# A decode step of windowed attention with a gated MLP: w_q loaded in three transfers instead of one, fewer transfers at the end

## The chip, the core and the metric

One Trainium2 chip, one of its cores, one launch. The metric is device time in microseconds (us) of the whole program. The core has a matrix engine (PE, with its weight loads shown as PEld), three engines for elementwise work (DVE, ACT, POOL), SP, which here only issues transfers, and 16 DMA engines that move data between the chip's memory (HBM) and the 128 partitions of on-chip memory (SBUF).

## What is computed

Two sequences, one new token each, D = 512. Cut to what matters:

```python
xn = layernorm(x)                                  # x: 2 x 1 x 512
q = (xn @ wq).reshape(2, 1, 32, 128)               # wq: 512 x 4096
k, v = the last 4096 rows of k_cache, v_cache      # 2 x 8 heads x 32768 x 128, each head for 4 heads of q
s = softmax(q @ k.T * 128 ** -0.5) @ v @ wo        # wo: 4096 x 512
z = gelu(xn @ w_in); z1, z2 = halves of z          # w_in: 512 x 1792
g = silu((z1 * (w_sp * layernorm(z2) + b_sp)) @ w_out)   # w_out: 896 x 512
out = x + s * g
```

All is float32. The weights and the 4096 rows of 16 heads of K and of V make 89.4 MB, each byte of which is used once.

## The kernel before

All large loads go through one ring in SBUF of four slots of 4 MB (line 80, 32 KB in each partition). `enqueue` (line 85) puts a load in line for the next slot or slots; `advance` (line 92) marks slots as free and issues the loads whose slots are free, in order, from SP's queue. So the loads are issued in a fixed order, each as soon as the work that read its slot before is done: w_q in two slots (line 120), w_in (121) and w_out (122) in one each, then in turn a K and a V load of 4 MB for each of eight units (lines 155 to 159; a unit is two KV heads of one sequence), then w_o in three slots (lines 179 and 180).

A large load puts 128 rows into 128 partitions. `load_rows` (line 112) gives partition p four rows of w_q that lie next to each other in HBM, one run of 64 KB; 16 DMA engines with 8 of the 128 partitions each carry it. `load_blocks` (line 164) does the same for w_o, which is cut in 32 blocks: block j holds row 32p + j of w_o in partition p, 2 KB each, 256 KB in all. The first slot has 16 blocks in one transfer, the second 8, and the third is cut in transfers of 4, 1, 1, 1 and 1 blocks, so that the last matmuls wait for little. Once 16 blocks are in line, x is loaded a second time for the final addition, into rows of `x4` 16 partitions apart, one transfer for each sequence (lines 173 to 175). `by_group` (line 129) is the same layout of all eight rows in HBM as one pattern; the output is stored through it (line 555).

The order of the work on the engines is the program's order, kept by the helper on line 27 (so most records of the trace have its line, 37). ACT loads x (line 109) for the layernorm; lines 219 to 232 make `xnT`. The 32 matmuls of q (lines 263 to 271; the profile counts each as two) read all of w_q with all 128 partitions as the contraction, so they begin when all of w_q has landed; `advance(0, 1)` after them issues the first K loads. Then the gated MLP is done as far as `gate` (lines 293 to 363). The units follow (lines 486 to 515): DVE transposes K into `kt`, PE forms the scores, ACT the exponentials, PE the product with V (`acc`). Lines 516 to 531 finish the last two units into `oT`, the attention's result in columns.

The end is lines 534 to 555. PE multiplies `oT` with blocks 0 to 27 of w_o into `part`; ACT copies it to `parts`; PE adds blocks 28 and 29, then the shares in `parts`, then blocks 30 and 31 into `so`, in this order. DVE multiplies with `gate` and adds `x4`, and SP stores the result.

A transfer signals that it has landed through one of eight semaphores, which all transfers of the program take in turn; one that gets a semaphore again waits until the transfer that had it before has landed.

Of the kernel before, what the change touches and what calls it, by code (L numbers as in the profile page):

```python
# [14 lines left out]
P = 128  # L15
HQ, DH = 32, 128
G = 4
# [25 lines left out]
def kernel(  # L43
# [14 lines left out]
    pe, dve, act, sp = (InOrder(tc, e) for e in (nc.tensor, nc.vector, nc.scalar, nc.sync))  # L58
    B, _, D = x.shape
# [5 lines left out]
    KT = D // P  # L65
# [19 lines left out]
    def enqueue(load, count=1):  # L85

        at = turns[0] % 4
        turns[0] += count
        queue.append((load, range(at, at + count)))
        advance()  # L90

    def advance(*slots):
        for n in slots:
            free[n] = True
        while queue and all(free[n] for n in queue[0][1]):
            load, at = queue.pop(0)
            for n in at:
                free[n] = False
            load(ring[:, at[0] * SLOT : (at[-1] + 1) * SLOT], at[0])

    def const(name, *shape):
        return cst.tile([P, *shape], F32, tag=name, name=name)
# [7 lines left out]
    weight = {}  # L110

    def load_rows(name, w, k):
        def load(t, at):
            n = k * w.shape[1]
            sp.dma_start(t[:, :n], w.rearrange("(p k) f -> p (k f)", p=P))
            weight[name] = t[:, :n].rearrange("p (k f) -> p k f", k=k)

        return load

    enqueue(load_rows("q", wq, KT), 2)  # L120
    enqueue(load_rows("in", w_in, KT))
    enqueue(load_rows("out", w_out, FT))
    win, wout, wqt = (weight[n] for n in ("in", "out", "q"))
# [5 lines left out]
    def by_group(t):  # L129

        return bass.AP(tensor=t.tensor, offset=t.offset, ap=[[DC, G], [D, B], [1, DC]])
# [32 lines left out]
    def load_blocks(piece):  # L164
        def load(t, at):
            t = t.rearrange("p (j d) -> p j d", d=D)
            a = 0
            for n in piece:
                j = len(blocks)
                sp.dma_start(t[:, a : a + n, :], wo_v[:, j : j + n, :])  # L170
                blocks.extend((t, a + i) for i in range(n))
                a += n
            if len(blocks) == 16:
                for b in range(B):
                    sp.dma_start(x4[16 * b : P : 32, :], x[b].rearrange("o (g c) -> (o g) c", g=G))

        return load

    for piece in ((16,), (8,), (4, 1, 1, 1, 1)):
        enqueue(load_blocks(piece))  # L180


# [8 lines left out]
    x4 = const("x4", DC)  # L191
# [72 lines left out]
    for k in range(KT):  # L264
        for r in range(2):
            for g in range(G):
                c = (r * G + g) * 512
# [82 lines left out]
    for j in range(FT):  # L350
        g = j % G
# [111 lines left out]
    def gather(b):  # L463

        hq = sb.tile([P, 32], F32, tag="hq", name=f"hq{b}")
        by_d = col[0][32 * b : 32 * b + 32, :].rearrange("p (j d) -> p d j", j=NCH)
        for e in range(4):
            dve.reduce_sum(hq[32 * e : 32 * e + 32, :], by_d[:, 32 * e : 32 * e + 32, :], axis=AX.X)
        t = bank(f"oT{b}", "acc")[:, :32]
        pe.matmul(t, perm, hq, start=True, stop=True)  # L470
        return t
# [56 lines left out]
    t = gather(last.b)  # L528
# [7 lines left out]
    for n in range(EARLY):  # L536
        t, a = blocks[n]
        g = n % G
# [4 lines left out]
    for n in range(EARLY, 32):  # L543
        if n == LATE:
            spread_quarters(so, parts, start=False, stop=False)
        t, a = blocks[n]
# [37 lines left out]
```

## Time and profile before

| | us |
|---|---|
| median of 3 runs (217.4 to 217.73) | 217.57 |
| the profiled execution | 218.1 |
| its span, first to last instruction | 216.3 |
| PE busy in it | 149.5 |
| DVE busy | 107.1 |
| ACT busy | 43.5 |

The profile is of one execution, and its span starts at 0. Busy time is that of instructions; a DMA engine's time stands apart, as the share of the 16 engines' span. A chain entry "DMA tile<-tensor" lasts from the issue of a transfer to its landing; "issue" is time in which an engine waited for nothing that the profile shows. The granted clock is the part of its full rate that PE was given. Where bytes per time are shown for very short slots, a packet is counted whole in the slot in which it starts.

### The profile page before, as it was taken

The page shows a single profiled execution, that of the slowest core. Times are in us where ns is not written, and L with a number is a line of the kernel's source. Part 1 is how long each engine was busy: PE and PEld are TensorE (multiplying, and loading weights), DVE is VectorE, ACT ScalarE, POOL GpSimd, SP SyncE. Part 2 cuts the span into 40 slices and gives each one's busy share as a digit, 9 for nine tenths or more (in the row PEclk, how much of TensorE's full clock was granted, in tenths as well). Part 3 has the DMA queues.
Part 4 walks back from the last instruction along what each step waited for, and adds up shares of the span by engine and source line. Part 5 has one row for each costly group of instructions (what it writes and reads, how often), then busy time and mean ns, then how long its engine had stood idle before and what let it go on. Part 6 is the DMA issues. An engine that isn't in the chain of part 4 may idle for free.

```text
span 216.3 us, 2178 instructions
## 1 busy us (share of the span) xinstructions
PE 149.5 (69%) x848; PEld 41.7 (19%) x848; DVE 107.1 (50%) x160; ACT 43.5 (20%) x107; POOL 4.2 (2%) x22
## 2 busy tenths in 40 slices
PE   0100796417199499499599779829968977987793
PEld 0100222111012122122122122202212221222221
DVE  2400016430895890792694449487459089233101
ACT  5000000241022214212411511411241151241001
POOL 6100000000000000000000000000000000000000
PEclk9999996965559979969969969976996997999678
DMA  9988999999999999999999999999999999999980
GB/s 376 400 388 388 424 427 458 445 424 430 442 414 454 394 467 403 448 418 454 418 435 430 418 448 412 439 424 448 412 448 421 436 424 436 430 430 409 417 346 17
DMA packets 3789, 89.54 MB, mean 414 GB/s; under 512 B 434, under 2 KB 450, under 8 KB 964
## 3 DMA queue, kind: packets, MB, share of 16 engines
q1 hardware_dynamic: 3772, 89.40, 96.5%
q8 instruction: 7, 0.11, 0.2%
q14 instruction: 2, 0.02, 0.0%
q10 hardware_dynamic: 8, 0.00, 0.0%
HBM read 89.40 MB, written 0.00 MB: 413 GB/s over the span
## 4 chain that ended last, share of the span: by engine, by line
PE 55%; DMA 25%; DVE 15%; ACT 2%; issue 2%; DVEq 0%; ACTq 0%
PE s L37 15%; DMA ring<-in_A_wo_dram 15%; PE sh L37 12%; PE acc L37 11%; DMA ring<-in_A_wq_dram 10%; DVE kt L37 8%; PE q_ps L37 4%; PE part L37 4%; PE col L37 2%; PE z L37 2%; PE y L37 2%; PE mo L37 1%; DVE gate L37 1%; DVE u L37 1%; DVE qm L37 1%
## 5 line engine op out<-in xcount | busy, mean ns | idle before, releaser
L37 DVE STREAM_TRANSPOSE kt<-ring 128x2048 f32<-128x2048 f32 x32 | 72.1, 2284 | 10.7 <-DMA ring<-in_A_k_cache_dram 10.7
L37 PE MATMUL sh<-kt,qbd 128*32 128x512 f32 x256 | 41.9, 666 | 24.4 <-DVE kt L37 24.4
L37 PE MATMUL s<-shs,add_dq 128*128 128x512 f32 x64 | 41.5, 755 | 0.0
L37 ACT ACTIVATE shs<-sh 128x512 f32<-128x512 f32 x32 | 19.1, 597 | 97.2 <-PE sh L37 97.2
L37 PE MATMUL acc<-ring,pT 128*32 128x512 f32 x256 | 33.1, 646 | 0.0
L37 PE MATMUL q_ps<-ring,xnT 128*32 128x512 f32 x64 | 9.3, 746 | 15.5 <-DMA ring<-in_A_wq_dram 15.5
L37 DVE TENSOR_REDUCE m<-s 128x2 f32<-128x512 f32 x8 | 5.5, 685 | 22.5 <-PE s L37 22.5
L37 PEld LDWEIGHTS s<-shs,add_dq 128*128 128x128 f32 x64 | 11.2, 219 | 27.6 <-issue 23.2
L37 PEld LDWEIGHTS sh<-kt,qbd 128*32 128x32 f32 x256 | 7.2, 112 | 43.8 <-issue 35.3
L37 PEld LDWEIGHTS acc<-ring,pT 128*32 128x32 f32 x256 | 7.8, 119 | 25.5 <-issue 19.4
L37 DVE STREAM_TRANSPOSE qT<-q_ps 128x512 f32<-128x512 f32 x2 | 1.4, 718 | 22.8 <-PE q_ps L37 22.7
L37 PE MATMUL part<-ring,oT 128*32 128x512 f32 x56 | 9.2, 825 | 1.4 <-DMA ring<-in_A_wo_dram 1.4
L37 ACT ACTIVATE o<-acc,diag 128x128 f32<-128x128 f32 x30 | 8.6, 374 | 4.9 <-PE acc L37 4.9
L37 ACT ACTIVATE p<-s,nb 128x256 f32<-128x256 f32 x16 | 7.6, 487 | 6.8 <-DVE nb L37 6.6
L37 ACT ACTIVATE zs<-z 128x448 f32<-128x448 f32 x1 | 0.5, 544 | 34.5 <-PE z L37 34.5
L37 PE MATMUL col<-o,sel 128*32 128x512 f32 x14 | 7.3, 601 | 0.0
L37 PEld LDWEIGHTS q_ps<-ring,xnT 128*32 128x32 f32 x64 | 2.5, 134 | 21.4 <-issue 21.4
L37 PE MATMUL y<-ring,hT 128*32 128x512 f32 x14 | 3.6, 1058 | 3.8 <-DVE hT L37 3.8
L37 DVE TENSOR_TENSOR res<-so,gate 128x128 f32<-128x128 f32 x1 | 0.3, 292 | 11.7 <-PE so L37 11.7
L37 DVE STREAM_TRANSPOSE pT<-p 128x512 f32<-128x512 f32 x8 | 5.4, 674 | 1.2 <-ACT p L37 1.2
L37 ACT ACT_TABLE_LOAD x4 | 5.1, 1283 | 1.9 <-issue 1.9
L37 PE MATMUL xnT_ps<-ident,xn 2*128 2x2 f32 x4 | 0.6, 252 | 6.8 <-DVE xn L37 6.8
(112 smaller groups left out, 64.0 us busy)
## 6 DMA issues: line engine op xcount, KB each, us to landing
ring<-in_A_k_cache_dram SPq DMA_DIRECT2D x8, 4096.0 KB, 19.0
ring<-in_A_v_cache_dram SPq DMA_DIRECT2D x8, 4096.0 KB, 25.0
ring<-in_A_wo_dram SPq DMA_DIRECT2D x1, 4096.0 KB, 31.8
ring<-in_B_w_in_dram SPq DMA_DIRECT2D x1, 3584.0 KB, 30.0
ring<-in_A_wo_dram SPq DMA_DIRECT2D x1, 2048.0 KB, 27.2
ring<-in_B_w_out_dram SPq DMA_DIRECT2D x1, 1792.0 KB, 33.9
ring<-in_A_wo_dram SPq DMA_DIRECT2D x1, 1024.0 KB
ring<-in_A_wo_dram SPq DMA_DIRECT2D x4, 256.0 KB, 17.2
```

What stands on the lines that cost most here:

```text
L37: return self.tc.keep_in_program_order(call(*args, **kwargs))
```

## The change

w_q is loaded in three transfers. The first has partitions 0, 4, 8, ..., the second 2, 6, 10, ..., the third all odd ones: 32, 32 and 64 of the 128 rows of 64 KB, which makes 2, 2 and 4 rows for each of 16 DMA engines. x for the result comes in one transfer of eight rows. In the third slot of w_o, the first two of the four single blocks come in one transfer.

```diff
-    enqueue(load_rows("q", wq, KT), 2)
+    def load_q(t, at):
+
+        rows, n = wq.rearrange("(p k) f -> p (k f)", p=P), KT * wq.shape[1]
+        for first, step in ((0, 4), (2, 4), (1, 2)):
+            sp.dma_start(t[first:P:step, :n], rows[first:P:step])
+        weight["q"] = t[:, :n].rearrange("p (k f) -> p k f", k=KT)
+
+    enqueue(load_q, 2)
...
             if len(blocks) == 16:
-                for b in range(B):
-                    sp.dma_start(x4[16 * b : P : 32, :], x[b].rearrange("o (g c) -> (o g) c", g=G))
+                sp.dma_start(x4[0:P:16, :], by_group(x))
...
-    for piece in ((16,), (8,), (4, 1, 1, 1, 1)):
+    for piece in ((16,), (8,), (4, 2, 1, 1)):
         enqueue(load_blocks(piece))
```

The program has as many transfers as before: two more at its start, one fewer for x and one fewer for w_o.

## The prediction

> **What bounds the kernel now.** I read the page first: the span, the strip of 40 slices and the queues.
>
> ```profile
> span 216.3 us, 2178 instructions
> PEclk9999996965559979969969969976996997999678
> DMA  9988999999999999999999999999999999999980
> q1 hardware_dynamic: 3772, 89.40, 96.5%
> ```
>
> The reader is to see one digit repeated: the 16 DMA engines are busy from the first slice to the last but one, and queue 1, SP's own, has 96.5% of their time. No compute engine comes near. So I ask next whether the DMA engines ever wait. The table by stage answers it (after the times: busy time of PE, PEld, DVE, ACT and POOL, then the granted clock, the DMA share and GB/s; a packet counts whole where it starts, so shares over 1 in a short stretch only mean that many started there).
>
> ```profile
> 1.10:1.70 0.60, 0.00 (x0) 0.00 (x0) 0.26 (x1) 0.00 (x0) 0.59 (x3) 1.00 0.07 7
> 1.70:2.10 0.40, 0.00 (x0) 0.00 (x0) 0.31 (x2) 0.23 (x1) 0.40 (x5) 1.00 3.46 1147
> 2.10:2.50 0.40, 0.00 (x0) 0.00 (x0) 0.00 (x0) 0.40 (x1) 0.40 (x3) 1.00 4.02 1475
> 5.00:22.40 17.40, 0.61 (x4) 0.55 (x4) 2.30 (x13) 0.33 (x2) 0.76 (x4) 1.00 0.99 429
> 31.00:200.00 169.00, 129.37 (x690) 34.54 (x683) 102.11 (x138) 39.96 (x102) 0.00 (x0) 0.85 1.00 431
> 207.00:209.60 2.60, 2.60 (x24) 0.72 (x20) 0.00 (x0) 0.00 (x0) 0.00 (x0) 0.75 1.02 392
> 209.60:211.70 2.10, 2.10 (x36) 0.84 (x28) 0.00 (x0) 0.13 (x1) 0.00 (x0) 1.00 0.44 167
> ```
>
> Before 1.7 us nothing of queue 1 moves; from 5 to 200 us the share is 0.99 to 1.00 at 429 to 431 GB/s; from 209.6 us it falls, because engines finish one by one. **The kernel is a full pipe with a start of about 2 us and an end of about 4.5 us**, and only three things can move its time: when the pipe starts, what it loses on the way, and what comes after the last bytes. The chain in order of time shows the two ends (start, length, what):
>
> ```profile
> 0.74 22.00 DMA ring<-in_A_wq_dram
> 22.73 0.14 issue
> 22.87 9.32 PE q_ps L37 x64
> ...
> 170.30 31.85 DMA ring<-in_A_wo_dram
> 202.15 0.14 issue
> 202.28 9.21 PE part L37 x56
> ...
> 211.57 0.61 ACT parts L37
> ...
> 212.22 0.91 PE so L37 x24
> ...
> 213.15 0.30 DVE res L37
> ...
> 213.48 0.29 DVE res L37
> ```
>
> w_q is first in the pipe, and its landing lets PE begin. The 16-block load of w_o lands at 202.15 us; from there PE, ACT and DVE run to the end. An earlier pipe moves both.
>
> **w_q in three transfers.** The bytes stay the same, and all of w_q is still needed before the first q matmul, since the contraction runs over all partitions. So nothing is gained by an early part. What can be gained is the start. Below, the first packets of the pipe: the stretch 1.7 to 2.5 us in slots of 20 ns (3277 is one 64 KB packet that starts there), and then the second packets, 4.7 to 5.6 us in slots of 22.5 ns.
>
> ```profile
> GB/s 0 3277 3277 3277 0 0 0 0 0 0 3277 0 3277 3277 0 0 0 3277 0 0 0 3277 3277 3277 0 3277 0 0 3277 0 0 0 3277 0 3277 0 3277 3277 0 0
> GB/s 0 0 0 0 0 0 2913 0 2913 0 2913 5825 0 0 2913 2913 5825 2913 2913 0 5825 0 0 0 2913 0 0 0 0 2913 0 0 0 0 2913 0 0 0 0 0
> ```
>
> The 16 engines do not start together: the first at 1.72, the last at 2.44 us, about 48 ns apart. Each then has 8 rows of w_q waiting. 128 rows in 0.72 us are 5.6 ns a row, as if the rows were handed out one engine after another. The only other start on an empty queue is the output's, 8 rows (512 B packets, slots of 57.5 ns from 214 us):
>
> ```profile
> GB/s 0 0 0 0 0 0 0 0 0 0 0 0 0 0 0 0 0 9 53 9 0 0 0 0 0 0 0 0 0 0 0 0 0 0 0 0 0 0 0 0
> ```
>
> Its 12 packets (8 of data, 4 of semaphores) start within three slots, so 8 rows take some 0.1 us, at most 14 ns a row. With 32 rows in the first transfer the handing out should take 32 x 5.6 = 0.18 to 32 x 14 = 0.45 us. The last engine then starts at 1.9 to 2.17 instead of 2.44 us: 0.27 to 0.54 us earlier; the mean engine gains half of that.
>
> Is the head start kept? The second packets start between 4.83 and 5.48 us, 0.65 apart where the first were 0.72 apart. A 64 KB row takes 65536 B / (429/16 GB/s) = 2.44 us, yet from the first starts to the second it is some 3 us: the first bytes come about 0.6 us late, for a reason that no row shows and that an earlier start may not move. So part of the head start can be lost there. Bounds: 0 (all lost) to 0.54 us. Every landing waits for the slowest engine, so its gain counts more than the mean's; I take **0.30 us**, a little under the middle of the last engine's gain.
>
> What else the split issues:
>
> ```profile
> 0.74 0.38 SPq L37 DMA_DIRECT2D ring<-in_A_wq_dram  x1
> 1.18 0.41 SPq L37 DMA_DIRECT2D ring<-in_B_w_in_dram  x1
> 1.63 0.48 SPq L37 DMA_DIRECT2D ring<-in_B_w_out_dram  x1
> 28.77 3.99 SPq L37 DMA_DIRECT2D ring<-in_A_k_cache_dram  x2
> ```
>
> Two more issues on SP, 0.44 us each, put w_in and w_out 0.9 us later in SP's queue, to 2.1 and 2.5 us. Their cover is w_q's data, which keeps the engines busy to 22 us. The second transfer is issued near 1.2 us, and the first keeps each engine for two rows, 4.9 us; so no engine runs dry between them. ACT's load of x shares these first microseconds; its consumers (layernorm, xnT) are done by 8 us and PE waits for w_q until 22.7. The first q matmul has three landings to wait for in place of one; two come long before. Should that add 0.1 us on PE, q ends later and so do the k loads queued behind it at 28.77 us, while the pipe still has w_out to move: nothing.
>
> **w_o: two single blocks in one transfer.** A 2 KB row takes longer than its bytes: at the singles the table has 392 GB/s at a share of 1.02, so 2048 B / (384/16) = 85 ns a row, against 76 ns at 431 GB/s, 9 ns for each packet. Joining two blocks saves 8 packets an engine: **0.07 us** at the last landing. Blocks 28 and 29 now land together, at the time of 29; PE takes them after its 28 blocks of `part`, at 211.26 us in the row below, later than that. The bounds are 0 and 0.07.
>
> **x for the result** is 8 rows of 512 B either way, one issue fewer. It is needed 40 us later by the last addition: nothing.
>
> **A wait goes.** SP's own waits and the last issue of w_o (the last column is issue to landing):
>
> ```profile
> SPq L37 <- DMA ring<-in_A_wo_dram: 7.6, 1, 7.6
> ring<-in_A_wo_dram SPq DMA_DIRECT2D x1, 256.0 KB, 10.0
> 211.26 0.63 PE L37 MATMUL so<-ring,oT 128*32 128x128 f32 x16
> ```
>
> The last block's issue stands 7.6 us until the 16-block load has landed, since the transfers take eight semaphores in turn and it is the eighth after that load. With two transfers fewer at the end it looks back to a V load that has long landed and is issued near 194 us. But at 202.16 us the queue still held up to 15 blocks, 3.9 MB or 9 us, and the block landed 10.0 us after its issue, in the stream's own order. So this too is worth nothing; at most a few hundredths if the tail has a gap that I can't see.
>
> **Sum.** 0.30 + 0.07 = 0.37 us. The profiled execution took 218.1 us (span 216.3, 1.8 around it) and would take 217.7; the median of the runs, 217.57, is 0.5 lower, and from it I get **217.2 us**. No step works on 0.2% (0.44 us, about what a measurement of this kernel can tell from no change) with certainty: the likeliest gain is just under it.
>
> **Rivals.**
>
> *The rows of a small transfer meet at one door (slower).* Every large transfer in this trace goes to all 128 partitions, and every engine keeps its pace of 27 GB/s. No row shows a transfer to 32 partitions with a step. If there two engines write through one entrance of SBUF at the same time, each goes at half pace. w_q's 8.39 MB take 19.5 us at 431 GB/s; at half pace the pipe is late by up to 19.5 us, by 4.9 if only the first 32 rows suffer; everything behind shifts, since the pipe has no slack: 222.5 to 237 us. It decides as soon as w_q lands over 0.5 us later than 22.7. [...] Chance 0.17.
>
> *The head start is lost.* The first packets wait longer for their bytes instead of starting earlier, or the start of an engine doesn't depend on the rows. 0.0 to 0.15 us remain: 217.5. For it: the second packets' spread above. Chance 0.18.
>
> *A new wait.* If the three transfers, whose partitions interleave, were held apart (each waiting for the one before to land), each would cost a start of 1.0 us from issue to first packet and up to 0.7 for the last engine: 2.0 to 3.4 us, 219.6 to 221. Against it: the two loads of x interleave in the same way and follow each other without a wait.
>
> ```profile
> 170.69 1.21 SPq L37 DMA_DIRECT2D x<-in_A_x_dram  x2
> ```
>
> Two issues of 0.6 us in 1.21 us leave no room for one. Chance 0.03.
>
> *More than the head start.* PE runs the 28 blocks at a granted clock of half for two steps:
>
> ```profile
> 201.45:204.86 3.41, 2.58 (x15) 0.74 (x19) 0.05 (x1) 0.00 (x0) 0.00 (x0) 0.50 0.97 411
> 204.86:208.28 3.42, 3.42 (x24) 0.93 (x20) 0.00 (x0) 0.00 (x0) 0.00 (x0) 0.50 0.99 405
> ```
>
> The first step is 76% busy (2.58 of 3.41) and the clock stays low; an earlier landing fills it further, and if that lifts the clock at 204.86 us, `part` ends 1.7 us earlier. Then the last block's landing (202.16 + 10.0 = 212.16 us) sets the end: its 8 matmuls are half of the 0.62 us after 212.47, so they start at 212.78 now, 0.6 later than they could. The median lies 0.5 below the profiled execution, so most runs may have this already. I give 216.8 and a chance of 0.07.
>
> **How the numbers follow.** The forecast has 0.55: gains of 0.15 to 0.7 us, 216.9 to 217.4. The range runs from the last rival's 216.7 to 217.9, a little above the lost head start and the spread of the runs; the door and the new wait, 0.20 together, are left out, as their times are far off. Faster by over 0.2%: 0.25 of the 0.55 and the 0.07, 0.32. Within: 0.29 and 0.17, 0.46. Slower: the 0.20, and 0.02 from the edges, 0.22.
>
> **What would show it.** Right: first packets spread over 0.2 to 0.45 us, w_q landed by 22.45, the 16 blocks of w_o near 201.85, the last single block issued near 194 us with no landing waited for. Wrong: w_q landing later than 22.7 with a DMA share near 0.5 before it (the door), gaps in SP's first issues (a new wait), or an earlier first packet with w_q's landing unmoved (head start lost).

## The result: slightly slower, and a start that comes later

| | before | after |
|---|---|---|
| median of 22 runs, us | 217.57 | 217.96 |
| ratio of the times, 95% interval | | 1.002, 1.001 to 1.0029 |
| the profiled execution, us | 218.1 | 217.93 |
| its span, us | 216.3 | 216.0 |

The change costs 0.39 us, 0.1 to 0.3%; the forecast was a gain of 0.37, and the time lies 0.06 us above the range. Two profiles alone would have told the opposite: the profiled execution of before took 0.5 us more than the median. So the times are compared by medians, and the profiles only at places where executions hardly differ, above all the first microseconds. Two executions in a slower state of the chip, one of `covered` below and one of before beside `late_start`, are left out of the medians and ratios. A ratio is estimated by itself and need not be the quotient of the medians beside it.

There the difference is plain. First SP's issues after the change (start, length, times merged), then the stretches around the first packets, as they were read before, then the first packets of 64 KB in slots of 20 ns from 1.7 us.

```profile
0.74 1.89 SPq L37 DMA_DIRECT2D ring<-in_A_wq_dram  x3
2.67 0.59 SPq L37 DMA_DIRECT2D ring<-in_B_w_in_dram  x1
3.30 0.43 SPq L37 DMA_DIRECT2D ring<-in_B_w_out_dram  x1
```

```profile
1.70:2.10 0.40, 0.00 (x0) 0.00 (x0) 0.31 (x2) 0.17 (x1) 0.40 (x5) 1.00 1.01 328
2.10:2.50 0.40, 0.00 (x0) 0.00 (x0) 0.36 (x1) 0.40 (x1) 0.40 (x3) 1.00 5.95 1966
5.00:22.40 17.40, 0.61 (x4) 0.55 (x4) 2.28 (x13) 0.00 (x0) 0.76 (x4) 1.00 1.01 437
31.00:200.00 169.00, 128.59 (x683) 33.25 (x676) 101.20 (x135) 39.64 (x102) 0.00 (x0) 0.86 1.00 431
```

```profile
GB/s 0 0 0 0 0 0 0 0 0 0 0 0 0 0 0 0 0 0 0 6554 3277 9830 0 0 3277 3277 0 0 0 0 0 6554 0 0 3277 3277 0 0 3277 3277
```

The reader is to see that the first packet starts at 2.08 us, where it was 1.72: not earlier but **0.36 us later**. And the last two of the 16 engines start at 2.70 and 2.74 us, after the end of the row, where the last was at 2.44: the starts spread over 0.66 us, where it was 0.72. Three issues in 1.89 us are 0.63 from one to the next, where w_q's one issue took 0.38. From 5 us on the stream is as full and as fast as before. The chain in time order has the two ends:

```profile
0.74 0.57 SPq L37
1.37 0.57 SPq L37
1.98 20.97 DMA ring<-in_A_wq_dram
23.09 8.39 PE q_ps L37 x64
```

```profile
195.37 16.91 DMA ring<-in_A_wo_dram
212.28 0.04 issue
212.33 0.47 PE so L37 x8
```

w_q lands at 1.98 + 20.97 = 22.95 us (before 22.74), 0.21 us later, and the last block at 212.28 (before 212.16). Why w_q's landing moved by less than the first packet no row shows. The last block is now issued at 195.37 us without waiting for the first part of w_o; `tail_only` below shows that this brings nothing the runs can tell, as forecast.

### The profile page after: what moved, and what is told of

Read it like the earlier page. It is cut to its first block, busy times and chain, and to the rows that moved or that the text cites. A ratio compares the mean times of both kernels' runs of the same rounds, so it can differ in the third digit from the quotient of the medians.

```text
span 216.0 us, 2181 instructions
## 1 busy us (share of the span) xinstructions
PE 147.8 (68%) x848; PEld 39.8 (18%) x848; DVE 107.3 (50%) x160; ACT 43.5 (20%) x107; POOL 4.2 (2%) x22
## 4 chain that ended last, share of the span: by engine, by line
DMA 40%; PE 34%; DVE 20%; issue 2%; ACT 2%; SPq 1%; DVEq 0%
DMA ring<-in_A_k_cache_dram 23%; DVE kt L37 13%; DMA ring<-in_A_wq_dram 10%; PE sh L37 9%; PE s L37 9%; DMA ring<-in_A_wo_dram 8%; PE acc L37 6%; PE q_ps L37 4%; PE y L37 2%; PE z L37 1%; SPq L37 1%; PE mo L37 1%; PE col L37 1%; DVE gate L37 1%; DVE u L37 1%
## 5 line engine op out<-in xcount | busy, mean ns | idle before, releaser
L37 DVE STREAM_TRANSPOSE kt<-ring 128x2048 f32<-128x2048 f32 x32 | 72.3, 2287 | 23.6 <-DMA ring<-in_A_k_cache_dram 23.3
L37 PE MATMUL s<-shs,add_dq 128*128 128x512 f32 x64 | 39.4, 723 | 0.0
L37 PE MATMUL acc<-ring,pT 128*32 128x512 f32 x256 | 36.2, 698 | 0.0
L37 PE MATMUL q_ps<-ring,xnT 128*32 128x512 f32 x64 | 8.4, 681 | 16.1 <-DMA ring<-in_A_wq_dram 16.1
L37 PEld LDWEIGHTS s<-shs,add_dq 128*128 128x128 f32 x64 | 10.4, 203 | 28.4 <-issue 24.0
L37 PEld LDWEIGHTS acc<-ring,pT 128*32 128x32 f32 x256 | 8.4, 128 | 27.6 <-issue 24.7
L37 DVE STREAM_TRANSPOSE qT<-q_ps 128x512 f32<-128x512 f32 x2 | 1.4, 718 | 22.5 <-PE q_ps L37 22.4
L37 PE MATMUL part<-ring,oT 128*32 128x512 f32 x56 | 8.0, 730 | 0.7 <-DVE oT L37 0.7
```

The source lines that it names most:

```text
L37: return self.tc.keep_in_program_order(call(*args, **kwargs))
```

## The experiments

**Theory.** A transfer whose rows aren't one plain run takes longer to issue; put first, it starts the whole stream later, and since the stream is full to the end, the time is later by as much. **Rivals:** the loss comes from the joined transfers at the end; or from three issues in a row, whatever their shape; or from the fewer rows of the first transfer; or from something that stepped transfers do to the stream later. All edits are to the kernel before unless the text says otherwise, and each time stands beside runs of before on the same chip.

### Each part alone

`split_only` has the change's first part, the three stepped transfers of w_q, and before's end. `tail_only` has the other two parts.

> Only w_q in three transfers; the end as before. Start theory (the stepped transfer of 32 partitions takes longer to issue, 0.575 us where the 128-partition one took 0.380, and the whole stream starts 0.35 us later): first issue again near 0.57 us, first packet near 2.09 us, w_q landed near 22.95 us, time 0.35 to 0.5 us above before, as much as the change or 0.07 more. End theory (the loss comes from the joined blocks or the one load of x): time within 0.15 us of before.

> Only the end changed: x in one transfer, blocks 28 and 29 in one; w_q in one transfer. Start theory: first packet at 1.74 us, w_q landed at 22.74, time 0 to 0.1 us below before; from the landing of the 16-block load to that of the last block 9.90 us as after the change, 9.97 before. End theory: 0.3 to 0.5 us above before.

Measured: split_only 218.09 us beside 217.56, ratio 1.0022 (1.0009 to 1.0034); tail_only 217.64 beside 217.56, ratio 1.0004 (0.9995 to 1.0013). First the first packets of split_only, then those of tail_only, in the slots used above:

```profile
GB/s 0 0 0 102 0 0 0 0 0 0 0 0 0 0 0 0 0 0 0 6554 6554 0 3277 3277 6554 0 3277 0 3277 6554 3277 0 3277 3277 0 0 0 0 0 0
```

```profile
GB/s 0 0 0 9830 3277 0 0 3277 3277 0 3277 6554 6554 0 3277 0 0 0 0 0 0 0 3277 0 0 0 0 0 0 0 3277 0 0 0 0 0 3277 0 0 0
```

2.08 us with the split (the 102 ahead of it is x), 1.76 without. The split alone costs as much as the whole change, within the noise; the end theory falls. The joined blocks' 0.07 us is too small for these runs to show.

### Three transfers of another shape

`columns` cuts w_q in three transfers as well, but by columns, each to all 128 partitions; `blocks` by partitions that lie together.

```diff
-        for first, step in ((0, 4), (2, 4), (1, 2)):
-            sp.dma_start(t[first:P:step, :n], rows[first:P:step])
+        for lo, hi in ((0, n // 4), (n // 4, n // 2), (n // 2, n)):    # columns
+            sp.dma_start(t[:, lo:hi], rows[:, lo:hi])
...
+        for lo, hi in ((0, 32), (32, 64), (64, P)):                    # blocks
+            sp.dma_start(t[lo:hi, :n], rows[lo:hi])
```

> w_q again in three transfers of a quarter, a quarter and a half of the bytes, but each to all 128 partitions (16, 16 and 32 KB of each row); the end as before. Start theory, with the partition step or the 32 rows as the cause of the slow issue: first issue 0.38 to 0.45 us, first packet near 1.74 us, time within 0.15 us of before. Count theory (three issues in a row delay the start, whatever their shape): first packet later than 1.9 us, time 0.3 us or more above before.

> w_q in three transfers of 32, 32 and 64 partitions that lie together, without a step; the end as before. If the step makes the issue slow: first issue near 0.4 us and first packet near 1.75 us. If it is that the transfer has not all 128 partitions: issue near 0.57, first packet near 2.09 us, as with the step. Apart from this, if partitions that lie together share an entrance of SBUF, the first transfers go at half pace: w_q lands 10 to 20 us later (33 to 43 us) and the time is 10 to 20 us above before; if not, w_q lands near 22.7 to 23.0 us.

Measured: columns 217.63 us beside 217.56, ratio 1.0008 (0.999 to 1.0027); blocks 238.68 us, ratio 1.0985 (1.0965 to 1.1004). SP's three issues in columns, and its first packets, now of 16 KB (819 is one):

```profile
0.73 1.38 SPq L37 DMA_DIRECT2D ring<-in_A_wq_dram  x3
```

```profile
GB/s 0 819 1638 0 819 0 0 0 0 819 819 2458 0 0 819 0 819 0 922 819 0 819 0 819 0 0 819 0 0 0 0 0 0 0 0 0 0 0 0 0
```

Of blocks, the three issues (shortest, median and longest in ns), the first packets of 64 KB, the stretch in which w_q is on its way, and w_q's last transfer in the chain:

```profile
L37 SPq DMA_DIRECT2D ring<-in_A_wq_dram x3: 394/397/561, 0.7 to 1.6; - x3
```

```profile
GB/s 0 0 3277 6554 3277 3277 3277 3277 0 6554 6554 0 6554 0 0 0 3277 0 0 0 0 0 0 0 0 0 0 0 3277 0 0 0 0 0 0 0 0 0 0 0
```

```profile
5.00:22.40 17.40, 0.61 (x4) 0.55 (x4) 2.28 (x13) 0.00 (x0) 0.75 (x4) 1.00 1.12 230
```

```profile
1.63 42.01 DMA ring<-in_A_wq_dram
```

Both start at 1.72 to 1.74 us, though the first transfer of blocks has 32 rows: neither the number of transfers nor 32 rows in the first one delays the start. With blocks, 15 of the 16 first packets are in the row, from 1.74 to 2.26 us, and one comes after it: 32 rows in the first transfer don't bring the engines together. And blocks shows the half pace that the prediction's rival of the door has a price for: engines as busy as ever (share 1.12) at 230 in place of 429 GB/s, and w_q lands at 1.63 + 42.01 = 43.64 us, 21 us later. That the rows meet at one entrance of SBUF no row shows.

### The step, on either side

`step_sbuf` keeps the steps in SBUF and reads rows that lie together in HBM; `pairs_hbm` is one transfer to all partitions in order whose source goes in 64 pairs with a long step, like the K loads.

```diff
+        for first, step, lo in ((0, 4, 0), (2, 4, 32), (1, 2, 64)):    # step_sbuf
+            sp.dma_start(t[first:P:step, :n], rows[lo : lo + P // step])
...
+        sp.dma_start(t[:, :n], wq.rearrange("(s i k) f -> i s (k f)", s=2, k=KT))    # pairs_hbm
```

> w_q in three transfers whose rows go to every 4th, every 4th and every 2nd partition as in the change, but come from 32, 32 and 64 rows that lie together in HBM (so rows of w_q stand in other partitions than the reference needs: q is left wrong; the work is the same). If the step in SBUF makes the issue slow: first issue near 0.575 us, first packet near 2.09 us. If the step in HBM does: first issue near 0.40, first packet near 1.75 us. [...]

> w_q in one transfer to all 128 partitions, whose source rows are 0, 256, 4, 260, and so on: 64 pairs with a long step, the same shape of source as the K loads (rows of w_q stand in other partitions than the reference needs: q is left wrong). If only a step in SBUF is slow: issue 0.38 to 0.45 us, first packet near 1.75 us. If any pattern that isn't one plain run of rows is slow: issue 0.53 us or more as for the K loads (0.535), first packet near 2.05 us.

Measured, one time each (218.88 and 218.66 us, from which nothing is read). The issues of w_q and the first packets, of step_sbuf and then of pairs_hbm:

```profile
L37 SPq DMA_DIRECT2D ring<-in_A_wq_dram x3: 568/580/646, 0.7 to 2.0; - x3
```

```profile
GB/s 0 0 0 0 0 0 102 0 0 0 0 0 0 0 0 0 0 0 0 3277 3277 0 6554 6554 3277 0 0 3277 0 0 0 0 3277 3277 0 0 3277 0 0 0
```

```profile
L37 SPq DMA_DIRECT2D ring<-in_A_wq_dram x1: 666/666/666, 0.7 to 0.7; - x1
```

```profile
GB/s 0 0 0 0 0 0 0 0 0 0 0 0 0 0 0 0 0 0 0 0 0 0 0 0 3277 13107 0 0 3277 3277 6554 3277 3277 0 3277 0 0 0 0 3277
```

A step in SBUF alone gives the change's numbers (0.58, 2.08 us); the pairs in HBM alone give 0.67 and 2.18 us, with all 128 rows in one transfer. Either side is enough.

### A late start of another kind, and a start that is covered

`late_start` has nothing stepped: SP loads one unread number ahead of w_q. `plain_first` is the change with the first quarter of w_q's columns loaded ahead of the steps in a plain transfer.

```diff
+    sp.dma_start(scr, bass.AP(tensor=w_sp.tensor, offset=w_sp.offset, ap=[[1, 1], [1, 1]]))    # late_start
     enqueue(load_rows("q", wq, KT), 2)
...
+        sp.dma_start(t[:, : n // 4], rows[:, : n // 4])                                        # plain_first
         for first, step in ((0, 4), (2, 4), (1, 2)):
-            sp.dma_start(t[first:P:step, :n], rows[first:P:step])
+            sp.dma_start(t[first:P:step, n // 4 : n], rows[first:P:step, n // 4 :])
```

> The kernel before with a load of one number (4 bytes, not read by anything) issued by SP ahead of w_q; nothing else. Start theory: w_q's issue comes 0.25 to 0.6 us later, and the first packet and the time are later by the same amount, within 0.15 us: 0.25 to 0.6 us above before, although the bytes, the shape of w_q's transfer and the end are unchanged. If the start doesn't set the time (slack somewhere behind it): within 0.15 us of before.

> The change, with the first quarter of each row of w_q (16 KB) taken out of the three stepped transfers and loaded ahead of them in one plain transfer to all 128 partitions. w_q lands at the usual time, so the compute chain isn't late, and the stepped issues lie beside the plain transfer's 4.8 us of data. If the change loses by its late start alone: first packet near 1.74 us and time within 0.15 us of before, although each stepped issue still takes about 0.57 us. If the stepped transfers cost something beside the start: 0.3 us or more above before.

Measured: late_start 218.05 us beside 217.62, ratio 1.001 (0.9996 to 1.0023); plain_first 217.49 beside 217.62, ratio 0.9994 (0.9982 to 1.0006). The first packets of late_start, then the four issues of plain_first and its first packets of 16 KB:

```profile
GB/s 0 0 0 0 0 0 0 0 0 0 0 0 0 0 0 0 0 0 0 0 0 0 9830 0 6554 0 0 0 6554 3277 3277 3277 0 0 0 6554 3277 0 0 0
```

```profile
L37 SPq DMA_DIRECT2D ring<-in_A_wq_dram x4: 386/571/593, 0.7 to 2.4; - x4
```

```profile
GB/s 0 0 819 0 1638 0 0 819 1638 0 0 819 1638 819 0 0 819 0 0 2458 0 0 819 0 0 0 0 0 0 0 0 0 0 0 0 0 0 0 0 819
```

late_start's first packet is 0.42 us late and its median 0.43 (the interval of the times doesn't rule out no change, but the spans do: its 12 lie between 216.0 and 216.5 us, the 22 of before beside it between 215.5 and 215.9). plain_first has its stepped issues as slow as ever (median 0.57 us), the first packet at 1.74, and the loss is gone: its interval lies below the change's. So the steps cost nothing beside the start that these runs can tell, and the start passes through to the end about one to one.

### More on the cause, and two that missed

`two_steps` is the change with two stepped transfers of 64 rows. `quiet` and `alone` ask whether ACT's load of x, issued at the same moment as w_q, slows SP: ACT first runs an activation, in alone on the very tile that x is loaded to. `covered` is the change with w_out issued ahead of w_q and w_in after it.

> The change with w_q in two stepped transfers of 64 rows (partitions 0, 2, 4, ..., then the odd ones) in place of 32, 32 and 64. If the step delays the start whatever the rows: first issue 0.57 to 0.65 us, first packet 2.05 to 2.2 us, time 0.3 to 0.5 us above before, as for the change. If a first transfer of fewer rows helps the engines to start together and so makes up for a part: first packets spread more widely than with 32 rows (0.67 and 0.50 us there), and the time 0.1 us or more above the change's 217.96.

> The kernel before, with ACT held for its first table load (1.28 us) by an activation on a tile set to 1, so that ACT's load of x is issued at about 2.3 us instead of 0.73, after SP's first issues. If ACT's issue at the same moment slows SP's: w_q's issue 0.30 us or less, first packet 1.6 us or earlier, time 0.1 to 0.2 us below before. If not: issue 0.38 us, first packet 1.74 us, time within 0.1 us of before. xnT is then ready near 10 us, still long before w_q.

> The kernel before, with ACT's load of x made to wait for an activation that writes its tile first (after the table load of 1.28 us), so that no issue of ACT lies beside SP's first ones; the earlier run meant for this moved ACT's issue by 0.16 us only. If ACT's issue at the same moment slows SP's: w_q's issue 0.33 us or less, first packet 1.65 us or earlier, time 0.1 to 0.2 us below before. If not: issue 0.38 to 0.40 us, first packet 1.73 to 1.78 us, time within 0.1 us of before.

> The change, with one thing moved: w_out (one plain transfer to 128 partitions) is issued ahead of w_q's three transfers, w_in after them; slots of the ring as before. If the change loses by its late start alone, the loss goes: first packet near 1.74 us though w_q's issues still take about 0.57 us each, w_q landed near 27 us, and the time within 0.15 us of before (217.4 to 217.7). If the stepped transfers cost something beside the start (in the stream or later), the time stays 0.3 us or more above before. The first K load is then issued near 33 us, 1.5 us before the stream has nothing left; if that is too late, a gap in the DMA share near 34.5 us would show it.

Measured: two_steps 217.89 us beside 217.62, ratio 1.0011 (0.9997 to 1.0025), median of the spans 216.1 beside 215.7, first packet at 2.10 us; so the start is late with 64 rows as with 32, and the step is what counts. quiet 217.47 beside 217.62, ratio 0.9995 (0.9979 to 1.0011): a miss, ACT issued its load at 0.89 us, while its table was still loading. alone 217.58 beside 217.50, ratio 1.0008 (0.9993 to 1.0023); its rows:

```profile
0.73 0.39 SPq L37 DMA_DIRECT2D ring<-in_A_wq_dram  x1
2.68 0.52 ACTq L37 DMA_DIRECT2D xs<-in_A_x_dram  x1
```

With ACT out of the way SP's issue takes as long as before: ACT doesn't slow it.

covered was meant as what plain_first then was, and told something else: 220.62 us, ratio 1.0164 (1.0145 to 1.0183). Its start is early (1.76 us), SP issues the first K load at 32.83 us as expected, and the stream stays full to 200 us, but w_q lands at 27.23 us. DVE's waits for K, and then the shares of the chain that ended last by engine, both of covered:

```profile
DVE kt L37 <- DMA ring<-in_A_k_cache_dram: 3.5, 2, 2.3
```

```profile
PE 64%; DVE 17%; DMA 11%; ACT 3%; issue 2%; SPq 1%; DVEq 0%; ACTq 0%
```

Before, DVE waited 10.7 us for K, after the change 23.3; here 3.5, and the chain is PE's and DVE's. It seems that the work that follows w_q is itself nearly as long as the stream and, 4.5 us later, ends last; as `covered` moves three loads at once, no run shows the late w_q alone to do it.

No version beats before: columns, tail_only, quiet, alone and plain_first all have intervals that hold 1.

## Why the prediction was wrong

**The bound was right.** A full pipe whose start passes through to the end: late_start (first packet 0.42 us later, time 0.43) and plain_first (first packet at 1.74 us, time 217.49 beside 217.62) show both directions.

**The step that failed** is "128 rows in 0.72 us are 5.6 ns a row, as if the rows were handed out one engine after another", with what hung on it: "the last engine then starts at 1.9 to 2.17 instead of 2.44 us", and the bounds "0 (all lost) to 0.54 us", which left out a loss. Two things were assumed and not looked for. One, that the spread of the first packets is set by the rows; tail_only, whose first transfer is before's, spreads 15 of them from 1.76 to 2.42 us and one after 2.5, and blocks, with a quarter of the rows, spreads them no less; in the change the last engine starts at 2.74 us. What does set the spread stays open. Two, that a new transfer's first packet comes as soon after its issue as the old one's. It comes 0.36 us later, since the rows are stepped (0.32 to 0.36 against all runs in which a large plain load is issued first: they start at 1.72 to 1.76). The term of +0.30 us is in truth -0.36, which the change's 0.39 and split_only's 0.53 us agree with.

The trace of before held the warning. The issues by line, shortest, median and longest in ns:

```profile
L37 SPq DMA_DIRECT2D ring<-in_A_k_cache_dram x8: 534/535/655, 28.8 to 149.9; - x8
L37 SPq DMA_DIRECT2D ring<-in_A_wo_dram x7: 328/335/432, 170.3 to 202.2; - x7
L37 SPq DMA_DIRECT2D ring<-in_A_wq_dram x1: 380/380/380, 0.7 to 0.7; - x1
```

K's loads and the first part of w_o have the same 128 rows of 32 KB, but K's source is 64 pairs with a long step, and takes 535 ns to issue, where that part of w_o took 0.34 us (the 335 ns are the median of all seven loads of w_o). I counted the new issues at 0.44 us each, the plain loads' pitch, and let only the stretch behind them count, where they are hidden; the first of them stands ahead of everything. The traces show this much: 0.19 us more of issue came with 0.36 us more to the first packet. Where the other 0.17 goes no row shows; that stays open.

**The rivals.** "The head start is lost" is nearest, but there was none to lose. A new wait: none came. The door's half pace didn't come in the change (437 GB/s from 5 to 22.4 us), and did come in blocks: with 32 and 64 partitions that lie together it moved 230 GB/s, and the 21 us that this cost are near the upper price given. That price was worked out from the bytes and the pace in the trace of before; the entrance of SBUF in it was my assumption, and no run shows what halves the pace. The stepped rows kept the engines at full pace, 437 GB/s; how they are divided among the engines no row shows.

"More than the head start" named what sets the two profiled executions apart. These are the stretches from 200 to 207 us, before and after, with the granted clock as the third number from the end:

```profile
200.00:207.00 7.00, 5.59 (x32) 1.99 (x34) 0.55 (x2) 0.00 (x0) 0.00 (x0) 0.60 0.96 404
200.00:207.00 7.00, 5.21 (x32) 1.95 (x36) 1.34 (x5) 0.32 (x2) 0.00 (x0) 0.76 0.97 410
```

With the lower clock the 28 blocks of before were done at 211.49 us only, and the work on them set the end; with the higher one the landing of the last block, at 212.28, set the end, as that rival had it, and the span came out 0.3 us shorter in spite of the late start. What raised the clock no run shows.

**The end.** The last single blocks are issued early and nothing comes of it; the joined blocks and the one load of x are worth less than the runs can show, as forecast.

## What to carry to other kernels

In this kernel, whose DMA stream is full from end to end, the first issue was on the path (with it 0.19 us longer, the change took 0.39 us more), and the others, issued while the stream ran, were not (plain_first has three stepped issues of about 0.57 us behind a plain one, and 217.49 us beside 217.62). In one like it, make the first transfer the plainest there is, one run of rows to all 128 partitions, and put anything stepped or paired behind it. Before pricing a new transfer, compare issue times of the same size and different patterns in the trace at hand. And with a bound by the stream, ask how far the compute chain is behind it: here, with w_q landed 4.5 us later, the chain ended last.

## What the runs showed of the hardware beside this

- With a step in the access pattern, in SBUF (after, two_steps, step_sbuf) or in HBM (pairs_hbm), SP's first issue took 0.57 to 0.67 us in place of 0.38 to 0.40 for a large plain load, and the first packet started 1.34 to 1.44 us after the issue's begin in place of 0.98 to 1.03. Only first issues tell this: behind others a plain one was as long, the longest of the three in blocks 0.56 us.
- ACT's sequencer issued a load while ACT's table loaded: in quiet the load of x went out at 0.89 us, within a table load from 0.73 to 2.01 us.
- From 5 to 22.4 us, transfers to 32 or 64 partitions with steps of 4 and 2 ran at the full pace of 128 partitions (after and two_steps 437 GB/s, step_sbuf 425, before 429); to 32 and 64 that lie together at about half (blocks 230).
